# Two stores cut by rows instead of by columns, and a re-paired last row tile, at the end of a cross-network kernel

## Chip, cores, metric

One core of one Trainium2 chip. The metric is the device time of one execution in microseconds.

## Reference

```python
B, F, D, L = 16384, 26, 16, 6        # rows have Din = 416 features, bf16
def reference(x0, ws, bs):
    x = x0
    for l in range(L):
        proj = jnp.einsum('bd,de->be', x, ws[l]) + bs[l]
        x = x0 * proj + x
    return x
```

## The kernel before

The 16384 rows are 8 groups of 2048. A group is held transposed on the chip (features on partitions): three tiles of 128 features and one of 32. PE multiplies, ACT moves PSUM to SBUF and adds the bias, DVE multiplies by x0 and adds x, SP issues the transposes and nearly all stores. A DMA has "landed" when its semaphore tells that all of its data has arrived. A finished group has to be turned back to rows. For groups 0 to 6 the DMA engines do it (one transpose per tile, into the tile `ost`), and a plain DMA writes `ost` to memory. The last group (7) is not turned: its last layer is computed with rows on partitions, in 4 row tiles (`kk`) of 4 x 128 rows, each stored as soon as it is added. What the change moves lies in the last 18 us of the program; before that the work is the same.

Output of a group. `LAST - 1` is group 6, the last one that is turned by DMA:

```python
def output(g):
    s, s3 = xset[(g, L)], xtail[(g, L)]
    def turn(t):                      # transpose tile t: 2048 rows x 128 features
        add("sp", lambda h: h.dma_start_transpose(
            ost[:, :, t * P:(t + 1) * P], xs[s][:, t * GC:(t + 1) * GC]),
            reads=[("x", s, t, j) for j in range(NJ)], writes=[("ost", t)], ...)
    turn(0)
    # ... 32-feature tile into ot3, spread into ost later by POOL or ACT
    turn(1)
    turn(2)
    if g < LAST - 1:
        store(g, 0, D, range(NT + 1))
    else:
        store(g, 0, 2 * P, (0, 1))    # columns 0-255: needs tiles 0 and 1 only
# ... later, after the 32-feature tile is spread:
store(LAST - 1, 2 * P, D, (NT - 1, NT))   # columns 256-415
```

The last row tile of group 7 (`nat_out` is ACT's PSUM to SBUF move of 128 rows x 416; `nat_mul` and `nat_add` are DVE's; the third argument is how many of the four blocks):

```python
for j in range(NJ):
    nat_full(kk, j, bks[kk][j], False)
    nat_out(kk, j, bks[kk])
    if j:
        first, n = ((0, 2), (2, 1), (3, 1))[j - 1]
        nat_mul(kk, first, n)
        nat_add(kk, first, n)
    if j == 2:
        nat_store(kk, 0, 3)           # SP: 384 rows
nat_store(kk, 3, 4, "act")            # ACT: 128 rows
```

## Time and profile before

| | before |
|---|---|
| time, median of 3 runs | 479.14 us (478.65 to 479.40) |
| PE busy | 97% of the span |
| last DVE add ends | 473.6 us |
| last store has landed | 477.1 us |

The head of the page and part 4, the chain of work that ended last:

```profile
span 477.6 us, 8343 instructions
...
PE 462.0 (97%) x3317; PEld 195.7 (41%) x3371; DVE 404.1 (85%) x696; ACT 342.3 (72%) x372; POOL 6.5 (1%) x15
...
## 4 chain that ended last, share of the span: by engine, by line
PE 92%; ACT 2%; DVE 2%; DMA 1%; issue 1%; ACTq 0%
```

The chain sees PE, ACT and DVE and almost no DMA. It ends with the last add (473.21 us in the list below), the last instruction that counts as work: the stores behind it, and the queue in which they stand, are not in it. The queue shows in other views. First the timeline of the end (start, duration, engine, line, operation; SPq and ACTq lines are issues of DMAs, and the duration of several merged ones includes the waits between them):

```profile
457.47 4.45 SPq L637 DMA_TRANSPOSE ost<-x  x2
...
459.13 1.57 PE L794 MATMUL ps<-wm,x 128*128 128x416 bf16 x8
...
462.02 3.85 SPq L671 DMA_DIRECT2D out_dram<-ost  x2
...
465.92 7.37 SPq L867 DMA_DIRECT2D out_dram<-x  x4
...
473.21 0.38 DVE L860 TENSOR_TENSOR x<-x,x 128x416 bf16<-128x416 bf16 x1
473.62 0.37 ACTq L867 DMA_DIRECT2D out_dram<-x  x1
```

The second line is the anchor: **t0** is the start of the first matmul of the row tiles (459.13 us).

Then the DMA view for 462 to 478 us. The first two rows are 40 slices of 0.4 us: busy tenths of the 16 DMA engines and GB/s.

```profile
DMA  9900299999999999999999999999999999910000
GB/s 255 76 1 8 38 288 288 348 348 347 301 266 343 292 268 250 252 238 241 244 242 240 268 304 331 333 331 333 333 333 331 333 333 331 333 48 6 0 0 0
DMA packets 7680, 3.78 MB, mean 236 GB/s; under 512 B 3583, under 2 KB 7679, under 8 KB 7679
...
q8 instruction: 1, 0.02, 0.4%
issues: line engine op xcount, KB each, median us to landing
...
out_dram<-ost SPq DMA_DIRECT2D x1, 1024.0 KB, 7.0
out_dram<-ost SPq DMA_DIRECT2D x1, 640.0 KB, 6.5
```

Two things are to be seen. From the sixth slice (464 us) to the 35th (476 us) there is no gap: the transposes of group 6 end, and stores follow back to back until the end of the program. And the slices three to five move almost nothing (1 to 38 GB/s): for about 1.4 us the transposes stand still. In that stretch stands the one "instruction" packet of the view, 16 KB on queue q8, which the trace has at 462.2 to 463.2 us.

The windows view puts numbers on these stretches (us, busy time of each engine, granted clock, DMA share, GB/s): the frozen stretch, the 512 B packets of columns 0-255, the 320 B packets of columns 256-415, and the 832 B packets of group 7.

```profile
462.45:463.85 1.40, 1.40 (x20) 0.71 (x19) 1.18 (x3) 1.38 (x4) 0.00 (x0) 1.00 1.44 20
...
464.75:468.10 3.35, 3.35 (x26) 1.57 (x25) 3.04 (x6) 2.89 (x7) 0.00 (x0) 1.00 1.18 312
468.10:470.80 2.70, 2.70 (x22) 1.23 (x21) 2.48 (x5) 2.09 (x5) 0.00 (x0) 1.00 1.28 243
471.00:475.75 4.75, 0.45 (x3) 0.03 (x1) 2.48 (x6) 0.99 (x2) 0.00 (x0) 1.00 1.11 327
```

The short packets move fewer bytes per us with the engines fully busy.

### The profile page before, as it was taken

How to read it: one execution, taken by the hardware profiler on the slowest of the kernel's cores; microseconds unless marked ns; L12 is line 12 of the kernel's file. 1: busy time of each engine (PE TensorE's matmuls, PEld its weight loads, DVE VectorE, ACT ScalarE, POOL GpSimd, SP SyncE). 2: the span in 40 equal slices, each digit the busy share in tenths (PEclk: the TensorE clock that was granted, in tenths of full speed). 3: DMA queues.
4: the chain of work that ended last, by engine and by line, in shares of the span. 5: the costliest groups of instructions: out<-in, count | busy, mean ns of one | idle time of the engine just before them, and what ended most of it. 6: DMA issues, size and time to landing. Idle time of an engine off the chain costs nothing.

```text
span 477.6 us, 8343 instructions
## 1 busy us (share of the span) xinstructions
PE 462.0 (97%) x3317; PEld 195.7 (41%) x3371; DVE 404.1 (85%) x696; ACT 342.3 (72%) x372; POOL 6.5 (1%) x15
## 2 busy tenths in 40 slices
PE   7999999999999999999999999999999999999994
PEld 5444444444444444444444444444444444444342
DVE  1888888888888888898889869888888888888896
ACT  3677777777777777777777777777777777777684
POOL 1000000000000000000000000000000000000000
PEclk9999999999999999999999999999999999999999
DMA  9966840630002377369309941980000038026899
GB/s 228 175 164 147 178 99 1 132 90 1 25 10 42 63 213 169 78 137 243 85 22 205 207 98 24 182 258 0 2 13 22 18 64 235 5 45 145 210 170 259
DMA packets 140379, 53.31 MB, mean 112 GB/s; under 512 B 114346, under 2 KB 139444, under 8 KB 140340
## 3 DMA queue, kind: packets, MB, share of 16 engines
q1 hardware_dynamic: 139592, 52.24, 49.2%
q10 hardware_dynamic: 748, 0.54, 0.4%
q8 instruction: 26, 0.43, 0.4%
q14 instruction: 13, 0.11, 0.1%
HBM read 5.97 MB, written 13.63 MB: 41 GB/s over the span
## 4 chain that ended last, share of the span: by engine, by line
PE 92%; ACT 2%; DVE 2%; DMA 1%; issue 1%; ACTq 0%
PE ps L456 75%; PE ps L477 7%; PE ps L497 6%; ACT tw L394 2%; DMA wm<-in_ws_dram 1%; PE ps L794 1%; PE ps L471 1%; DVE x L408 1%; DVE tw L403 1%; PE ps L488 1%; PE ps L561 0%; DVE x L860 0%; DVE x L854 0%; ACT x L565 0%; PE ps L805 0%
## 5 line engine op out<-in xcount | busy, mean ns | idle before, releaser
L394 ACT ACTIVATE tw<-ps,bias 128x1024 bf16<-128x1024 f32 (+1 forms) x295 | 299.8, 1071 | 119.8 <-PE ps L477 75.7
L456 PE MATMUL ps<-x,wm 128*128 128x512 bf16 x1638 | 371.9, 379 | 7.0 <-issue 3.7
L456 PEld LDWEIGHTS ps<-x,wm 128*128 128x128 bf16 x1692 | 158.9, 98 | 214.8 <-issue 29.8
L403 DVE TENSOR_TENSOR tw<-tw,x 128x1024 bf16<-128x1024 bf16 (+1 forms) x285 | 192.8, 685 | 53.4 <-ACT tw L394 53.0
L408 DVE TENSOR_TENSOR x<-tw,x 128x1024 bf16<-128x1024 bf16 (+1 forms) x285 | 182.1, 679 | 0.0
L477 PE MATMUL ps<-x,w 32*128 32x512 bf16 x512 | 39.2, 379 | 0.0
L497 PE MATMUL ps<-x,wm 128*32 128x512 bf16 x564 | 33.0, 380 | 0.0
L434 ACT ACTIVATE ts<-ps,bias 128x512 bf16<-128x512 f32 x47 | 28.8, 701 | 0.0
L438 DVE TENSOR_TENSOR x<-ts,x 128x512 bf16<-128x512 bf16 x47 | 18.6, 417 | 3.2 <-DMA x<-x 3.2
L497 PEld LDWEIGHTS ps<-x,wm 128*32 128x32 bf16 x564 | 13.8, 96 | 17.6 <-issue 5.3
L477 PEld LDWEIGHTS ps<-x,w 32*128 32x128 bf16 x512 | 7.8, 92 | 27.6 <-issue 27.1
L436 DVE TENSOR_TENSOR ts<-ts,x 128x512 bf16<-128x512 bf16 x47 | 18.6, 418 | 0.0
L664 POOL COPY ost<-ot 128x512 bf16<-128x512 bf16 x6 | 5.0, 836 | 424.1 <-DMA ot<-x 424.1
L568 DVE COPY x<-ps 128x512 bf16<-128x512 bf16 x4 | 1.7, 424 | 9.4 <-PE ps L561 9.4
L794 PE MATMUL ps<-wm,x 128*128 128x416 bf16 x48 | 9.5, 340 | 0.0
L848 ACT ACTIVATE x<-ps 128x416 bf16<-128x416 f32 x16 | 7.7, 532 | 2.0 <-PE ps L794 1.9
L565 ACT ACTIVATE x<-ps 128x512 bf16<-128x512 bf16 x8 | 4.2, 598 | 6.4 <-PE ps L561 6.4
L794 PEld LDWEIGHTS ps<-wm,x 128*128 128x128 bf16 x48 | 4.4, 98 | 4.1 <-issue 1.0
L488 PE MATMUL ps<-x,w 32*32 32x512 bf16 x188 | 5.9, 374 | 0.0
L471 PE MATMUL ps<-x,w 32*32 32x512 bf16 x208 | 5.6, 385 | 0.0
L561 PE MATMUL ps<-ident,x 128*128 128x128 bf16 x64 | 5.2, 241 | 0.3 <-ACT x L565 0.3
L854 DVE TENSOR_TENSOR x<-x,x 128x832 bf16<-128x832 bf16 (+1 forms) x9 | 4.9, 540 | 0.7 <-ACT x L848 0.6
(38 smaller groups left out, 35.1 us busy)
## 6 DMA issues: line engine op xcount, KB each, us to landing
out_dram<-ost SPq DMA_DIRECT2D x6, 1664.0 KB, 7.0
x<-in_x_dram SPq DMA_DIRECT2D x7, 416.0 KB, 8.0
x<-x SPq DMA_DIRECT2D x24, 96.0 KB, 2.2
wm<-in_ws_dram SPq DMA_DIRECT2D x5, 312.0 KB, 3.3
x<-x SPq DMA_DIRECT2D x22, 64.0 KB, 2.0
out_dram<-x SPq DMA_DIRECT2D x3, 416.0 KB, 5.5
out_dram<-ost SPq DMA_DIRECT2D x1, 1024.0 KB, 7.0
x<-ost SPq DMA_DIRECT2D x28, 32.0 KB, 2.4
```

The source lines that it names most:

```text
L394: add("act", lambda h, a=a, w=w, b0=b0: h.activation(tw[r][:, a * CH:(a + w) * CH], psum[:, b0 * CH:(b0 + w) * CH], ACT_F.Identity, bias=b ...
L403: add("dve", lambda h, a=a, e=e: h.tensor_tensor(tw[r][:, a * CH:e * CH], tw[r][:, a * CH:e * CH], x0s[s0][:, i * GC + a * CH:i * GC + e * ...
L408: add("dve", lambda h, a=a, e=e: h.tensor_tensor(xs[so][:, i * GC + a * CH:i * GC + e * CH], tw[r][:, a * CH:e * CH], src(i, a, e), ALU.ad ...
L434: add("act", lambda h: h.activation(ts[r][:, :], bank(b), ACT_F.Identity, bias=bias[:, 3, l:l + 1], scale=1.0), reads=[("ps", b), "bias"], ...
L436: add("dve", lambda h: h.tensor_tensor(ts[r][:, :], ts[r][:, :], x03, ALU.mult), reads=[("ts", r)] + tok0, writes=[("ts", r)], release=True)
L438: add("dve", lambda h: h.tensor_tensor(x3s[so][:, :], ts[r][:, :], res, ALU.add), reads=[("ts", r)] + rtok, writes=[("x3", so), ("x3", so, ...
L456: add("pe", lambda h, t=t, j=j: h.matmul(bank(banks[j]), wm[l][:, t, ecols], src(t, j, j + 1), start=(first and t == 0), stop=(not first a ...
L471: add("pe", lambda h, q=q, j=j, r=r, c=c, o=o: h.matmul(psum[o, banks[j] * CH:(banks[j] + 1) * CH], w3[l][q, i * P + c * T32:i * P + (c + ...
L477: add("pe", lambda h, q=q, j=j, r=r: h.matmul(bank(banks[j]), w3[l][q, ecols], src[q, :], start=first, stop=not first, tile_position=(r * ...
L488: add("pe", lambda h, l=l, b=b, s3=s3, ri=ri, qi=qi, ro=ro, qo=qo: h.matmul(psum[qo, b * CH:(b + 1) * CH], w3[l][qi, NT * P:D], s3[qi, :], ...
L497: add("pe", lambda h, t=t, j=j, src=src, l=l, b=b, ro=ro, qo=qo: h.matmul(psum[qo, b * CH:(b + 1) * CH], wm[l][:, t, NT * P:D], src(t, j, ...
L794: add("pe", lambda h, t=t: h.matmul(bank(b, n=D), xcol(t, j, kk), wm[l][:, t, :], start=(first and t == 0), stop=(not first and t == NT - 1)),
```

## The change

The intent: whole rows of 832 B in group 6's stores instead of pieces of 512 and 320 B, cut by rows (row halves `j` 0-1 and 2-3) so that there are still two stores; the last tile's transpose is cut the same way, so that the first half does not wait for the whole of it. In the last row tile, DVE multiplies blocks singly as they come from ACT and adds them in pairs, and the two last stores are equal.

```diff
-        def turn(t):
+        def turn(t, j0=0, j1=NJ):
             add("sp", lambda h: h.dma_start_transpose(
-                ost[:, :, t * P:(t + 1) * P], xs[s][:, t * GC:(t + 1) * GC]),
+                ost[:, j0 * KK:j1 * KK, t * P:(t + 1) * P], xs[s][:, t * GC + j0 * CH:t * GC + j1 * CH]),
 ...
         turn(1)
-        turn(2)
         if g < LAST - 1:
-            store(g, 0, D, range(NT + 1))
+            turn(2)
+            store(g, 0, NJ)
         else:
-            store(g, 0, 2 * P, (0, 1))
+            turn(2, 0, 2)
+            turn(2, 2, NJ)
 ...
-    store(LAST - 1, 2 * P, D, (NT - 1, NT))
+    store(LAST - 1, 0, 2)          # rows of j = 0, 1, all 416 columns
+    store(LAST - 1, 2, NJ)
 ...
         nat_out(kk, j, bks[kk])
-        if j:
-            first, n = ((0, 2), (2, 1), (3, 1))[j - 1]
-            nat_mul(kk, first, n)
-            nat_add(kk, first, n)
-        if j == 2:
-            nat_store(kk, 0, 3)
-    nat_store(kk, 3, 4, "act")
+        nat_mul(kk, j, 1)
+        if j % 2:
+            nat_add(kk, j - 1)
+            nat_store(kk, j - 1, j + 1, "sp" if j == 1 else "act")
```

(The rest is bookkeeping: dependencies per tile and half instead of per tile.)

More of the change, by code (lines that the diff above doesn't have):

```diff
@@ L297, in load_group @@
         add("sp", lambda h: h.dma_start_transpose(Tb, x0[rows, D - P:D]),
-            writes=[("ost", t) for t in range(NT + 1)], lane="Tb", batch=g)
+            writes=[("ost", t, j) for t in range(NT + 1) for j in range(NJ)], lane="Tb", batch=g)
         turn(1)
@@ L304, in load_group @@
             add("sp", lambda h, q=q, j=j: h.dma_start(x0s[s][q, XW:XW + CH], Tb[P - T32:P, j * CH:(j + 1) * CH]),
-                reads=[("ost", 0)], writes=[("x03q", s, j)], lane=f"x03_{s}", batch=g)
+                reads=[("ost", 0, 0)], writes=[("x03q", s, j)], lane=f"x03_{s}", batch=g)
         if turn_of(g, 1):
@@ L635, in output @@
         s, s3 = xset[(g, L)], xtail[(g, L)]
-        def turn(t):
+        def turn(t, j0=0, j1=NJ):
             add("sp", lambda h: h.dma_start_transpose(
-                ost[:, :, t * P:(t + 1) * P], xs[s][:, t * GC:(t + 1) * GC]),
-                reads=[("x", s, t, j) for j in range(NJ)], writes=[("ost", t)],
-                lane="ot" if g < LAST - 1 else f"ot_{t}", batch=g)
+                ost[:, j0 * KK:j1 * KK, t * P:(t + 1) * P], xs[s][:, t * GC + j0 * CH:t * GC + j1 * CH]),
+                reads=[("x", s, t, j) for j in range(j0, j1)], writes=[("ost", t, j) for j in range(j0, j1)],
+                lane="ot" if g < LAST - 1 else f"ot_{t}{j0}", batch=g)
         turn(0)
@@ L659, in spread @@
         sp_ = ot3[:, :, :].rearrange("p k (j f) -> p j k f", j=NJ)
-        kw = dict(reads=["ot3"], writes=[("ost", NT)])
+        kw = dict(reads=["ot3"], writes=[("ost", NT, j) for j in range(NJ)])
         if eng == "act":
@@ L664, in spread, with store @@
             add(eng, lambda h: h.tensor_copy(dst, sp_), **kw)
-    def store(g, f0, f1, ts):
-        rows = out[g * GC:(g + 1) * GC, f0:f1]
-        o = ost[:, :, f0:f1].rearrange("p (j k) f -> p j k f", j=NJ)
+    def store(g, j0, j1):
+        rows = out[g * GC + j0 * CH:g * GC + j1 * CH, :]
+        o = ost[:, j0 * KK:j1 * KK, :].rearrange("p (j k) f -> p j k f", k=KK)
         pat = "(j p k) f -> p j k f" if g == 0 else "(j k p) f -> p j k f"
-        add("sp", lambda h: h.dma_start(rows.rearrange(pat, j=NJ, k=KK), o),
-            reads=[("ost", t) for t in ts], writes=[("out", g, f0)], lane="out", batch=g)
+        add("sp", lambda h: h.dma_start(rows.rearrange(pat, j=j1 - j0, k=KK), o),
+            reads=[("ost", t, j) for t in range(NT + 1) for j in range(j0, j1)],
+            writes=[("out", g, j0)], lane="out", batch=g)
     x5f = x0s[s5][:, 0:XW + CH].rearrange("p (a f) -> p a f", f=D)
```

## The prediction

> **What bounds the kernel now.** The span is 477.6 us. Up to 459 us the change touches nothing: PE is busy 97% of the span at full clock. Only the end can move. There the chain of waits names DVE and ACT up to the last add (473.6 us), but the DMA packets tell another story. In order of time they leave no gap from 464.75 us (just behind group 6's last transpose) to 476: 2048 packets of 512 B (group 6's columns 0-255, to 468.1), 2048 of 320 B (to 470.8), 2048 of 832 B (last group); last packet's end 476.55, last landing 477.12. The windows view gives 312, 243 and 327 GB/s for the three stretches. The last group's first store, ready at 465.9, sits 3.0 us in its issue and lands at 473.2. So the end is set by queued store traffic and by when that traffic can start, not by DVE.
>
> **What the change does, costed.**
> 1. Group 6 goes out as 2048 rows of 832 B instead of 4096 pieces. Before: 3.35 + 2.7 = 6.05 us of queue time. 2048 packets of 832 B take 5.0 to 5.15 us in the same trace (the store at 440.2; the stretch 471 to 475.75). Estimate: 0.9 us less, all on the binding resource. The Trainium skill, "DMA: Bandwidth & Descriptors", section "Why small descriptors are slow", has a fixed overhead per packet as mechanism; the trace agrees in direction.
> 2. The first store now needs half of the last tile too, so it is issued later than 462.02. The first half transpose can be issued at 459.45, when SP is free (inputs added by 459.3; the whole tile: 459.95). Its packets follow the second tile's at about 460.9, end near 462.1 and land between 462.9 and 464.2. The doubt is a freeze at 462.4 to 463.9: transpose packets of 18 ns last 1.5 us beside a 16 KB instruction packet (likewise at 13, 267 and 301 us). PE's program does not change, so it comes again. If the first half lands before it, the stores start behind the second half, about 464.7 as now; if not, about 465.2 (landing plus 1.0 us, issue to first packet of the store at 439.22). Cost: 0 to 0.5 us.
> 3. Two transpose issues of about 1.4 us (16 blocks take 2.0, 4 blocks 1.2) instead of one of 2.0: nothing.
> 4. Last row tiles: DVE loses one 0.37 us add, and the singles fill waits for ACT. The last add ends near 473.2, the SP store goes at 472.0 instead of 472.9, ACT's carries 208 KB instead of 104. The queue is full until 475, so almost none of it shows.
>
> Sum: stores start at 464.7 to 465.2, 10.3 us of packets, last packet at 475.5 to 476.0 against 476.55.
>
> **Prediction.** 478.5 us against 479.14; eight times in ten between 477.8 and 479.2. Faster by over 2%: 0.5%; within 2%: 99%; slower: 0.5%.
>
> **What would show it.** Packets of the last 12 us all of 832 B, about 395 per us, no gap, the first at 464.6 to 465.3; a shorter issue of the first last-group store; last add near 473.2; last landing near 476.4; PE unchanged.
>
> **What would make it wrong.** The first half caught in the freeze and landing after 464.5, or a DMA gap between halves and stores, which eats the gain (479.1 to 479.4); a split transpose costing more than its share; a queue that drains early, so that the end is the last add plus some 3 us; run-to-run spread, 0.75 us before, as large as the effect.

## The result, and the profile after

Six runs of each kernel: 478.38 us median (477.67 to 478.72) after, 478.83 us (478.37 to 479.40) before. The ratio is 0.9989, with a 95% interval of 0.9976 to 1.0001. A ratio here is the mean time of one kernel's fast runs over the mean of the other's of the same rounds, so it is not quite the ratio of the medians. By time alone the two kernels are the same; the profile tells more.

The head of the page and the chain:

```profile
span 476.8 us, 8398 instructions
...
PE 467.7 (98%) x3371; PEld 195.6 (41%) x3371; DVE 404.0 (85%) x696; ACT 342.3 (72%) x372; POOL 6.8 (1%) x15
...
## 4 chain that ended last, share of the span: by engine, by line
PE 95%; DVE 2%; DMA 1%; ACT 1%; ACTq 0%; issue 0%
```

The span is 0.8 us shorter, but not all of that is the change. PE's larger busy time only means that this trace has all 3371 matmul records, where that of before lacks 54. The timeline shows t0 at 458.78, 0.35 us earlier:

```profile
457.12 6.17 SPq L637 DMA_TRANSPOSE ost<-x  x3
...
458.78 1.57 PE L796 MATMUL ps<-wm,x 128*128 128x416 bf16 x8
...
464.38 1.13 SPq L672 DMA_DIRECT2D out_dram<-ost  x2
465.55 6.52 SPq L869 DMA_DIRECT2D out_dram<-x  x4
...
472.23 0.59 DVE L862 TENSOR_TENSOR x<-x,x 128x832 bf16<-128x832 bf16 x1
472.85 0.41 ACTq L869 DMA_DIRECT2D out_dram<-x  x1
```

PE is level with the other trace at 5 us and 0.36 us ahead of it from 9 us on, by the same amount all the way, so this is the start of the program and not the change. From t0, the last add ends at 14.04 instead of 14.46 us, and the first store of group 6 is issued at 5.60 instead of 2.88 us.

The DMA view for the same 462 to 478 us:

```profile
DMA  9001996079999999999999999999999995000000
GB/s 13 1 9 22 280 264 127 0 241 356 349 295 341 352 354 304 362 356 320 345 352 343 354 339 312 349 341 327 337 335 325 331 337 156 8 0 0 0 0 0
DMA packets 5390, 3.69 MB, mean 231 GB/s; under 512 B 1294, under 2 KB 5390, under 8 KB 5390
...
out_dram<-ost SPq DMA_DIRECT2D x2, 832.0 KB, 5.0
```

The freeze is there again, in the first four slices. Then comes what was not there before: the eighth slice is empty. The transposes are done, and no store has begun. After it the stores run without a gap, at a higher rate than before. In the windows view (the freeze, the gap, group 6's stores, group 7's stores):

```profile
462.10:463.50 1.40, 1.40 (x20) 0.71 (x19) 1.18 (x3) 1.39 (x4) 0.00 (x0) 1.00 0.24 5
...
464.65:465.25 0.60, 0.60 (x6) 0.33 (x4) 0.49 (x2) 0.60 (x3) 0.00 (x0) 1.00 0.00 0
465.30:470.30 5.00, 5.00 (x40) 2.22 (x39) 4.72 (x10) 3.93 (x9) 0.00 (x0) 1.00 1.04 339
470.65:474.65 4.00, 0.44 (x3) 0.02 (x1) 2.10 (x5) 0.98 (x2) 0.00 (x0) 1.00 1.10 336
```

So the change trades a later start of the stores for a shorter queue. In us from t0, from the records of packets and semaphores in the traces:

| | before | after | difference |
|---|---|---|---|
| first packet of group 6's stores | 5.62 | 6.52 | +0.90 |
| from there to the landing of group 6's last store | 7.11 | 5.79 | -1.32 |
| from there to the last landing of all | 5.25 | 5.24 | -0.01 |
| last landing | 17.98 | 17.55 | -0.43 |

The first half of the last tile landed at t0+5.52, its store's first packet came 1.00 us later, and that is the +0.90. The third row already says that the new last row tile did nothing: the last add is 0.42 us earlier, and the end does not notice.

### The profile page after: what moved, and what is told of

It reads as the page before. It is cut to its first block, busy times and chain, and to the rows that moved or that the text cites. A ratio compares the mean times of both kernels' runs of the same rounds, so it can differ in the third digit from the quotient of the medians.

```text
span 476.8 us, 8398 instructions
## 1 busy us (share of the span) xinstructions
PE 467.7 (98%) x3371; PEld 195.6 (41%) x3371; DVE 404.0 (85%) x696; ACT 342.3 (72%) x372; POOL 6.8 (1%) x15
## 4 chain that ended last, share of the span: by engine, by line
PE 95%; DVE 2%; DMA 1%; ACT 1%; ACTq 0%; issue 0%
PE ps L456 77%; PE ps L477 7%; PE ps L497 7%; PE ps L796 1%; DMA wm<-in_ws_dram 1%; PE ps L471 1%; PE ps L488 1%; DVE x L408 1%; DVE tw L403 1%; ACT tw L394 0%; PE ps L561 0%; DVE x L862 0%; ACT x L565 0%; PE ps L807 0%; ACT x L850 0%; DVE x L856 0%
## 5 line engine op out<-in xcount | busy, mean ns | idle before, releaser
L456 PE MATMUL ps<-x,wm 128*128 128x512 bf16 x1692 | 379.4, 379 | 1.0 <-DMA wm<-in_ws_dram 1.0
L497 PEld LDWEIGHTS ps<-x,wm 128*32 128x32 bf16 x564 | 13.8, 96 | 17.6 <-issue 5.3
```

Source lines behind the costliest of these rows:

```text
L456: add("pe", lambda h, t=t, j=j: h.matmul(bank(banks[j]), wm[l][:, t, ecols], src(t, j, j + 1), start=(first and t == 0), stop=(not first a ...
L497: add("pe", lambda h, t=t, j=j, src=src, l=l, b=b, ro=ro, qo=qo: h.matmul(psum[qo, b * CH:(b + 1) * CH], wm[l][:, t, NT * P:D], src(t, j, ...
```

## The experiments

Two theories of the end were put against each other first, then the freeze was taken apart. All figures are us from t0; the last row tiles start there in every kernel. Times and ratios are against the kernel before in the same rounds. Each kernel was profiled once. How far such figures scatter can be seen in pairs that differ in the last row tile alone: the first store packet differs by 0.12 us between before and 2, by 0.05 between after and 1, and by 0.22 between 5 and 7.

| kernel | last tile landed (first half, or whole) | first store packet | group 6 landed | last add ends | last landing |
|---|---|---|---|---|---|
| before | 6.15 (whole; first store does not need it) | 5.62 | 12.73 | 14.46 | 17.98 |
| after | 5.52 | 6.52 | 12.31 | 14.04 | 17.55 |
| 1 stores only | 5.56 | 6.57 | 12.33 | 14.46 | 17.59 |
| 2 row tiles only | 6.26 (whole) | 5.74 | 12.85 | 14.05 | 18.09 |
| 3 after, last tile turned whole | 6.25 (whole) | 7.25 | 13.05 | 14.04 | 18.26 |
| 4 after + 97 no-ops | 4.11 | 5.11 | 10.98 | 14.05 | 17.54 |
| 5 after + 80 no-ops | 4.10 | 5.10 | 10.99 | 14.04 | 16.30 |
| 6 before + 80 no-ops | 5.23 (whole) | 4.51 | 11.77 | 14.45 | 17.04 |
| 7 stores only + 80 no-ops | 4.31 | 5.32 | 11.14 | 14.45 | 16.48 |
| 8 third + 80 no-ops | 5.07 (whole) | 6.06 | 11.85 | 14.05 | 17.13 |
| 9 after + 30 no-ops | 4.66 | 5.66 | 11.44 | 14.05 | 16.74 |

### 1. The stores without the new last row tile

```diff
 # the changed kernel
-        nat_mul(kk, j, 1)
-        if j % 2: ...
+        if j: first, n = ((0, 2), (2, 1), (3, 1))[j - 1] ...   # as before
```

> The changed kernel with the last row tiles as before (3/4 by SP, 1/4 by ACT, four adds). All times from t0, the start of the first full-width matmul of the last row tiles (459.13 before, 458.78 after), so that run-to-run shifts of the start drop out; the last landing is t0+17.99 before, t0+17.54 after. Theory Q (the store queue alone sets the end, as predicted): last landing t0+17.5 to 17.65, the row-tile part is worth nothing. Rival R (the even last stores fill the queue's ragged end; the runs of before and after differ by 0.3 us between the fall of the 832 B stream and the last packet): t0+17.75 to 17.95, so the row-tile part is worth 0.2 to 0.4. Time against before: Q -0.4 us, R -0.1.

Measured: last landing t0+17.59, 0.04 us behind the changed kernel. 478.20 us median of 5, before 478.60, ratio 0.9991 (0.9975 to 1.0006). Theory Q holds and R falls: the row-tile part is worth nothing here, although it ends the last add 0.42 us sooner.

### 2. The new last row tile alone

```diff
 # the kernel before
-        if j: first, n = ((0, 2), (2, 1), (3, 1))[j - 1] ...
+        nat_mul(kk, j, 1)
+        if j % 2: ...
```

> The kernel before with the new last row tiles alone. Queue of group 6 as before: 512 B, then 320 B, first packet t0+5.6. Q: last landing t0+17.9 to 18.0 as before, time equal to before within 0.1. R: t0+17.6 to 17.75, time 0.3 less.

Measured: last landing t0+18.09, no better than before, with the last add at 14.05. 479.00 us median of 6, before 478.60, ratio 1.0008 (0.9989 to 1.0028). The same verdict from the other side: a store that is ready earlier only stands in the queue longer (ACT's last store landed 4.01 us after its issue, against 3.49 in before).

### 3. Row halves, but the last tile turned whole

```diff
 # the changed kernel
-            turn(2, 0, 2)
-            turn(2, 2, NJ)
+            turn(2)
```

> The changed kernel with the last tile turned whole; the two row-half stores both wait for it. Theory: landing of the whole turn at about t0+6.1, first 832 B packet 1.0 us later at t0+7.1 (after: t0+6.5), last landing t0+18.1, so 0.55 us worse than the changed kernel and 0.1 worse than before: all of the packet gain lost to the later start. Rival (halving the turn is worth nothing, the freeze decides both): first packet within 0.15 us of the changed kernel's, last landing t0+17.5 to 17.7.

The GB/s row of 462.5 to 478.5 us of this run, 0.4 us a slice:

```profile
GB/s 228 13 2 10 77 290 223 0 0 0 129 354 354 277 349 354 350 316 360 347 333 347 356 335 345 316 348 341 331 331 339 333 331 331 331 271 15 0 0 0
```

The gap between transposes and stores is now three slices and a half: the first packet comes at t0+7.25, 1.00 us after the whole tile has landed. Last landing t0+18.26, 0.71 worse than the changed kernel (0.55 was expected) and 0.28 worse than before (0.1 expected). 479.32 us median of 6, before 478.60, ratio 1.0012 (0.9993 to 1.0032). Row stores alone, then, lose as much by starting late as they win by long packets; the halved transpose is what leaves something over.

### 4. The freeze moved, with 97 no-ops

The freeze was suspected of the 0.9 us. It comes with a 16 KB instruction packet. The trace of before shows this more than once: five of its 26 packets run beside 272 to 552 transpose packets, and in each of the five some of these last 0.98 to 1.66 us, where the median is 0.018. The other 21 meet 41 transposes or fewer, none over 0.02 us. There are 26 such packets in a run for 6763 PE instructions, one per 260 (in the trace of after, one per 256 from the first packet to the last). The Trainium skill, "Runtime: NRT & Kernel Launch", section "Instruction fetch mechanics", says that an engine's instructions are fetched in blocks of 16 KiB, that is 256 instructions, which fits. PE's program is the same in before and after, so the packet comes at nearly the same place (t0+3.10 and t0+2.79). No-ops on PE put it elsewhere:

```diff
+    spare = [1] * 97
 ...
         _, (g, l), i = it
+        if spare and n > 1:          # one ahead of each of the first 97 tiles
+            spare.pop()
+            add("pe", lambda h: h.nop(hint="spare", nofuse=True))
```

> The changed kernel with 97 no-ops on PE, one ahead of each of the first 97 tiles. The 16 KB instruction packet, one per 256 PE instructions, then comes 97 instructions earlier, at about t0-2 instead of t0+2.8, where no transpose is moving. Theory F (the freeze of the transposes comes from this packet): no transpose packet above 0.6 us at t0+2 to t0+5, first half lands at t0+3.5 to 4.1 (after: t0+5.5), first store packet t0+4.4 to 5.0 (after: t0+6.5), last landing then limited by the last add: t0+16.2 to 16.8, about 1 us better than the changed kernel. Rival (the freeze belongs to this place of the program: store issue or the PE's transposes): freeze still at t0+3 to t0+4.7, last landing t0+17.5. If the no-ops cost PE time, the distance from the start to t0 grows; expected under 0.3 us.

Two windows of this run, the one in which transposes had stood still and the last microsecond of the stores:

```profile
462.70:464.70 2.00, 1.63 (x24) 1.20 (x20) 2.00 (x6) 1.11 (x3) 0.00 (x0) 1.00 1.01 197
...
476.45:477.50 1.05, 0.00 (x0) 0.00 (x0) 0.00 (x0) 0.00 (x0) 0.00 (x0) 0.50 0.07 21
```

The first line (t0+2.0 to t0+4.0) shows 197 GB/s; in the frozen stretch before and after had 20 and 5: the freeze has gone with the packet, which now came at t0-5.9 (about t0-2 was expected). It has moved rather than vanished: at t0-4.5 to t0-3.4, in the first tile, transposes now last up to 1.12 us, and no store at the end is held up by that. The first half landed 1.4 us earlier and the first store packet came at t0+5.11, a little later than the 4.4 to 5.0 expected. But the last landing stayed at t0+17.54, where 16.2 to 16.8 was expected: that part of the theory failed. The second line tells why: at the end, a share of 0.07, one engine of sixteen, works alone for a microsecond. The next instruction packet had now fallen into the stores. The DMA view of 472 to 474 us has it:

```profile
q1 hardware_dynamic: 806, 0.64, 107.3%
q8 instruction: 1, 0.02, 2.9%
```

2.9% of 16 engines for 2 us is 0.92 us on one engine, and the one that trails at the end trails by about that much. 478.56 us median of 6, before 478.60, ratio 1.0004 (0.9983 to 1.0024).

### 5. 80 no-ops: both packets out of the way

```diff
-    spare = [1] * 97
+    spare = [1] * 80
```

> The changed kernel with 80 no-ops on PE instead of 97. With 97 the freeze of the transposes went away and the stores started 1.4 us earlier (t0+5.1), but the next instruction packet fell at t0+11.9 into the stores; one engine then trailed the others by about 1 us, and the last landing stayed at t0+17.54. Theory F2 (the trailing engine is that packet's doing): with 80 the earlier packet comes at t0-5 to t0-2, the next one after PE's end or not at all; no trailing engine; the end is set by the last add (t0+14.05) plus about 2.4 us: last landing t0+16.2 to 16.7. Rival (the stores themselves end raggedly, whatever the packet): t0+17.3 to 17.6. Time about 1 us under before, ratio 0.998.

The last two windows of this run (the stores' last 0.85 us, and the microsecond after), and the no-ops as the line view has them (duration minimum/median/maximum in ns):

```profile
473.00:473.85 0.85, 0.00 (x0) 0.00 (x0) 0.00 (x0) 0.00 (x0) 0.00 (x0) 1.00 0.75 254
473.85:474.85 1.00, 0.00 (x0) 0.00 (x0) 0.00 (x0) 0.00 (x0) 0.00 (x0) 0.72 0.00 0
```

```profile
L765 PEldq NOP  x80: 13/13/13, 22.5 to 275.5; - x80
```

No trailing engine, and no instruction packet from t0-3.8 to the end. The earlier packet came at t0-4.95, and the freeze with it, in the first tile. The GB/s row of 451 to 456 us, 0.125 us a slice, has it from the 24th slice on (t0-4.2 to t0-3.1):

```profile
GB/s 289 287 289 285 285 283 285 281 283 181 23 74 0 0 0 0 158 170 213 199 211 166 43 6 0 6 6 10 8 10 10 63 270 291 295 291 287 287 293 289
```

Last landing t0+16.30, 1.25 us before the changed kernel's, inside the expected 16.2 to 16.7. 476.86 us median of 6 (476.61 to 477.42), before 478.83, ratio 0.9960 (0.9945 to 0.9974). This kernel beats both. It is correct, and it computes exactly what the changed kernel does.

### 6. The kernel before with 80 no-ops

Edit: the same three lines of no-ops in the kernel before.

> The kernel before with the same 80 no-ops. If F2 holds, its transposes end at about t0+4.2, the 512 B and 320 B stores at about t0+10.4, and the last row tiles' stores are no longer behind a queue: the end is the last add (t0+14.46) plus 2.1 us, last landing t0+16.4 to 16.8, equal to the changed kernel with no-ops within 0.2; then the change's gain exists only because the freeze makes the queue late. Rival (the packet sizes matter by themselves): t0+17.1 to 17.5, keeping the 0.4 us distance to the changed kernel.

Measured: last landing t0+17.04, 0.94 better than before without them, but 0.74 behind experiment 5. Neither number was right: I had expected equality within 0.2 from F2, and the rival's 17.1 to 17.5 is missed by a little. What it settles is that the packet sizes count by themselves: group 6's stores take 7.26 us from first packet to landing against 5.89 in experiment 5, and the queue is still full when the last stores are issued. 477.81 us median of 6, before 478.83, ratio 0.9979 (0.9963 to 0.9994).

### 7. The stores without the new row tile, 80 no-ops

Edit: experiment 1 with the no-ops.

> The row-half stores without the new last row tiles (the first experiment's kernel), with 80 no-ops. The queue is not the limit then, so the row-tile part should show for the first time: ACT's store is issued at t0+14.49 instead of 14.07 but carries half as much (0.35 us less to move). Expected last landing t0+16.4 to 16.7, 0 to 0.2 behind the changed kernel with no-ops. If it is 0.4 behind, the add's end alone counts.

Measured: last landing t0+16.48, 0.18 behind experiment 5, where 0 to 0.2 was expected. This run's first store packet was itself 0.22 later, but in both runs the stream falls to about 20 GB/s before the last stores begin (t0+14.25 to 14.5 here, t0+14.75 to 15.0 in experiment 5), so that hardly reaches the end: ACT's store is issued 0.41 us later and lands 2.00 us after its issue, against 2.23. 476.81 us median of 6, before 478.83, ratio 0.9956 (0.9940 to 0.9972). The times of 5 and 7 do not differ. Even where the queue all but drains before the last stores, an add that ends 0.42 us earlier buys at most 0.2, because ACT's store then carries twice the rows.

### 8. The last tile turned whole, 80 no-ops

Edit: experiment 3 with the no-ops.

> The changed kernel with the last tile turned whole (third experiment) and 80 no-ops. Tells what halving the turn is worth where no freeze stands in it. With the freeze it was worth 0.7 us (last landing t0+18.26 against 17.55). Theory: the whole turn lands at t0+5.2 (as in the kernel before with no-ops), the first store packet comes 1.0 us later at t0+6.2 against 5.1, and as the queue then stays full to the end, the last landing is t0+17.2 to 17.4 against 16.30. Rival (the add at the end sets it, as in the fifth experiment): t0+16.3 to 16.6.

Measured: first store packet t0+6.06, last landing t0+17.13, 0.83 behind experiment 5 (0.9 to 1.1 was expected). 477.95 us median of 4, before 478.84, ratio 0.9989 (0.9946 to 1.0031). Beside experiment 6 (17.04) it repeats the finding of the third: long packets and a whole-tile wait cancel, with the freeze or without.

### 9. 30 no-ops, a control

Edit: 30 in place of 80.

> Control for the no-ops: the changed kernel with 30 of them, so that the instruction packet should come at about t0-1 to t0+1.5, still where the second tile or the first half is being moved. Theory F2 (only the packet's place counts): transposes of 1 us and more again, now earlier, the first half lands at t0+4.8 to 5.6, first store packet t0+5.8 to 6.6, last landing t0+16.9 to 17.6. Rival (any no-ops help, for another reason): t0+16.2 to 16.5 as with 80.

The GB/s row of 457 to 473 us (t0 is 457.64):

```profile
GB/s 109 216 203 217 246 78 4 10 104 282 289 283 287 262 73 60 356 356 349 306 324 360 350 306 368 354 354 345 300 362 354 333 327 337 333 337 329 329 335 331
```

The packet came at t0+1.07 and the freeze with it, at t0+1.35 to t0+2.85, now at the end of the second tile. So the freeze follows the packet to a third place. It cost less than I expected: the first half landed at t0+4.66 (4.8 to 5.6 expected) and the last landing was t0+16.74 (16.9 to 17.6 expected). The row shows how: after the freeze the transposes run at 282 to 289 GB/s, against 203 to 246 ahead of it, and most of the lost time is made up before they end, at t0+5.21 against 4.98 in experiment 5. In these runs a freeze is dear only where something waits for a landing inside it. 477.32 us median of 4, before 478.84, ratio 0.9961 (0.9929 to 0.9992).

## Why the prediction was right, and where its terms were off

The total was right: 478.5 us was put down and 478.38 measured, and the last landing moved by -0.43 us from t0. The total agrees better than the step does: 0.64 us was forecast (against 479.14, the median of three runs), and 0.45 lies between the medians of six. The picture behind it was right too: the end is set by a full store queue and by the time it can start. Point by point:

1. *"Estimate: 0.9 us less, all on the binding resource."* Mis-sized: it was 1.32 us, and 1.37 in the pair without a freeze in the last tiles (7.26 against 5.89 us). I took stretches of steady rate, each up to the first packet of the next size. Measured like this, group 6's stores took 6.05 us before and 5.03 after (by count, to the 2049th packet), a gain of 1.02. The other 0.30 shows up behind that: from the first packet of group 7 to the last of all it is 5.75 us before and 5.45 after. In the trace of before the sizes overlap: the last 512 B packet ended 0.20 us after the first 320 B one began, the last 320 B packet 0.37 us after the first 832 B one. So the short packets cost more than the stretch in which they run alone. The mechanism that the Trainium skill gives for short packets was taken on trust; the runs show that short packets cost time, not why.
2. *"Cost: 0 to 0.5 us."* This step failed: it was 0.90 us. The packets did nearly as forecast: by count, some 950 of the first half's 1024 transpose packets had begun by 462.1 us in the trace of after, when the freeze set in. The rest were caught. And I let a caught half land by 464.2 in the time of before, soon after the freeze ends; in fact it landed 0.7 us after the last slow packet had ended, at t0+5.52, which is 464.65 in that time. The other half of the step held exactly: landing plus 1.0 us to the first packet, in every kernel of the table whose first store waits for the last tile.
3. *"Two transpose issues of about 1.4 us [...]: nothing."* The issues took 1.74 and 2.41 us, with the freeze in the second, and stood in nobody's way. Halving is worth 0.71 us with the freeze and 0.83 without.
4. *"The queue is full until 475, so almost none of it shows."* Right: 0.04 us in experiment 1, none in experiment 2, although the add ended 0.42 us sooner as forecast (0.4).

The two mis-sized terms have opposite signs, and by luck they nearly cancelled: -1.32 + 0.90 = -0.42, where -0.9 + (0 to 0.5) was forecast. The sum line of the prediction does not follow from these terms: it puts the whole queue at 10.3 us, where it had been 11.8, and the last packet 0.55 to 1.05 us earlier. The queue took 10.48, and the last packet came 0.42 earlier from t0. So the total is less of a confirmation than it looks. Of the marks that I named in advance, "no gap" was wrong (0.68 us of empty queue, which I had listed under what could go wrong). The first packet at 465.30 and the last landing at 476.33 fit as well as they do only because this run's t0 came 0.35 us earlier. The rest held: 832 B packets alone, a shorter issue of the first last-group store (1.4 us instead of 3.0), PE unchanged.

The freeze belongs to the 16 KB instruction packet: it left the last tiles and turned up elsewhere as that packet was moved (experiments 4, 5 and 9). Why a packet on one engine holds the transposes on all of them is not shown. Of the 2.0 us between the medians of before and experiment 5, 1.68 lie in the distance from t0 to the last landing; the other 0.3 are not explained, and the start of the program alone varies by more than that between runs.

## What to carry to other kernels

Where stores end a program, follow the packets and not the chain of waits: a chain that ends in an add can hide a full queue, and then only what shortens the queue or starts it earlier counts, not what makes the last store ready sooner. Measure a piece of queue from its first packet to its landing, as a mean rate leaves out the ragged end where one size runs into the next. When a wait is moved to a new transfer, look at what else is in flight as that transfer ends; here an instruction fetch stood exactly there, and 80 no-ops of 13 ns each, which move it, were worth more than the change itself.

## What the Trainium skill lacked or had wrong

- "Runtime: NRT & Kernel Launch", section "Instruction fetch mechanics", calls the cost of crossing a 16 KiB boundary "mostly hidden". For PE, whose fetch it was, that held (busy for all of the 1.40 us of the freeze). What the page lacks is the cost to other DMAs: transposes in flight stood still for about 1.4 us beside such a fetch, and a fetch amid plain stores left one DMA engine about 1 us behind the others. Moving the fetches away from the end took the last landing from t0+17.55 to t0+16.30.
- "DMA: Bandwidth & Descriptors" has no word, in its section on DMA transposes or elsewhere that I found, on transposes being held up by an instruction fetch, nor on the rate behind the freeze (282 to 289 GB/s against 203 to 246 ahead of it in experiment 9; why is not shown).
- The same page, section "Latency and other measured facts", gives about 600 ns to the first byte of a DMA issued from SP. From the landing that released a store to that store's first packet the runs show 0.99 to 1.01 us, of which less than 0.1 is the wait for SP to issue. From the start of the issue it is 0.91 to 0.93 us, from its end 0.53 to 0.54. The page does not say from where it counts; from the end of the issue the runs agree with it.
- The same page says that short descriptors are slow, and the runs agree in direction. It gives a fixed overhead of about 3 cycles per packet, with an example of 256 B. By that rule (an estimate: 19 and 13 cycles against 29) the two pieces of a row would take 10% longer than the whole; here they took 23% longer: 2048 pieces of 512 B and 2048 of 320 B took 7.11 us from first packet to landing, the same bytes as 2048 rows of 832 B took 5.79.
